# Where an interleaved weight decoder keeps its intermediate words, and in which slots it runs

## The chip, the core and the metric

The kernel runs on one core of a Trainium2 chip. The metric is the device time of one execution in microseconds (us); the median of the runs of the kernel before is 1018.41 us.

## What is computed

Attention over 4 batches, 8 heads, 576 rows of 64 feeds a rational feed-forward layer, and that feeds a layer of eight routed experts. The change sits between the first two. Cut to that:

```python
scores = scale * q @ k.T                       # 4 x 8 x 576 x 576
scores = where(scores >= max - tau, scores, -1e9)
x = softmax(scores) @ v                        # rows of 512: x is 2304 x 512
h = x @ w_in                                   # 2304 x 2048
g = (a0 + a1*h + a2*h^2 + a3*h^3) / (1 + |b0|*|h| + |b1|*h^2 + 1e-6)
y = g @ w_out                                  # 2304 x 512
# then: gate by argmax, one of 8 experts (512 -> 1024 -> 512) per row
```

`w_in` and `w_out` arrive as 64-bit floats. [...]

## The kernel before

**Tiling.** `x` stands transposed in SBUF as 18 tiles of 128 rows. The feed-forward layer works in 96 chunks: a chunk is one group of three row tiles (`SEGS`) with one of 16 pieces of 128 hidden columns. A chunk's first product is 12 matmuls (L945), its second is 9 (L1017), five slots later (`G_LAG`). Chunks go in pairs through the rational function: ACT lines L968 to L970, POOL L971, ACT L980 and L981, DVE L959 to L961, ACT L998, POOL L999, and DVE L973 and L974. The PSUM tile of a pair's first product comes back with L961 of that pair; there are two such tiles.

**Slots.** `moe1` is a generator that advances one slot at a time. Slots 0 to 51 stand beside the last 52 of the 144 attention steps (`PRE`), slots 52 to 56 beside attention's end, and chunk c has slot 53 + c. Slot 54 is cut in three (`HALVES`), so that hooks at 54.5 and 54.75 fall between pieces of attention's end. Slot 57 (`END`) opens the pools of `w_out`'s split pieces and the last two PSUM banks (`ps_b`); slot 52 opens `ps_h` (the first products) and `ps_a` (two banks for sums of second products).

**Decoding.** The weights come in 32 pieces of 128 x 512 values, in the order of `STREAM`: (0, n) is piece n of `w_in`, (1, n) of `w_out`. A piece is loaded by an SP DMA into `raw`, its exponent is scaled by ACT (L621), and `step` runs three DVE operations: the low word's last bits (L618), the merge (L624), the sign (L628, into a `mag` tile). `sign` also issues the next load. The first eight pieces do this in place, `raw` to `raw` to `mag`, all in SBUF; from the ninth on (`late`) the intermediate words stand in one PSUM bank (`aux`), and for `w_out` POOL takes the last bits (L616) three slots ahead. A decoded `w_in` piece is summed (L800), the sums of two pieces go through a matmul (L809) and a row of tiny DVE operations (L634 to L653) to a scale, POOL makes factors of it (L834 to L839), and the piece is split in two halves of a product (ACT L846 and L847, or L849 and POOL L850; then POOL L851). A `w_out` piece is split by ACT L856 and POOL L857.

**What sets the order.** Every engine runs its queue in the order in which the program was written out, and that is set by tables: `FIRST_AT` (slots in which the first eight pieces are done), `EARLY_STEPS` (the three DVE operations of the first two pieces apart), `FIRST_EXPONENTS`, `EARLY_SUM` (the scale of pieces 0 and 1), `DEC_AT` and `DEC_EVERY` (a later piece every 1.6 slots from slot 59). Hooks of one slot run in a fixed order behind that slot's chunk work.

Of the kernel before, what the change touches and what calls it, by code (L numbers as in the profile page):

```python
# [13 lines left out]
I32 = mybir.dt.int32  # L14
# [39 lines left out]
END = 57  # L54
# [3 lines left out]
IN_LOAD = (8, 12, 33, 37, 41, 52, 52)  # L58
COEFFICIENTS = 30
STREAM = ((0, 0), (0, 1), (0, 2), (0, 3), (1, 0), (1, 1), (1, 2), (1, 3), (0, 4), (0, 5), (0, 6), (0, 7), (1, 4), (1, 5), (1, 6), (1, 7), (0, 8), (0, 9), (0, 10), (0, 11), (1, 8), (1, 9), (0, 12), (0, 13), (1, 10), (1, 11), (0, 14), (0, 15), (1, 12), (1, 13), (1, 14), (1, 15))  # L60
EARLY_STEPS = ((19, 21, 25), (27, 31, 33))
EARLY_SUM = 35
FIRST_AT = (25, 33, 52, 53, 55, 57, 57, 58)
FIRST_EXPONENTS = (17, 25, 46, 48, 50, 56, 56, 57)
SHIFT_LEAD = 3
SECOND_SUM = 54
HALVES = (54,)
DEC_AT = 59
DEC_EVERY = 1.6


def decode_at():
# [11 lines left out]
OUT_LAG = 1  # L84
# [582 lines left out]
def moe1(nc, tc, xT, vs, w_in, w_out, a, bb, w_gate, w_ogate, gates, ident, yd, part, L, consts, keep, side, early_bank):  # L667
# [43 lines left out]
    def at(slot, f, *args):  # L711
        hooks.setdefault(max(slot, 0), []).append((f, args))
# [7 lines left out]
    def run(slot):  # L720
        order = (load_next, last_bits, exponent, sum_in, red_in, clamp_red, split_out, split_in, scale_in, factors_in)
        for f, args in sorted(hooks.pop(slot, ()), key=lambda x: order.index(x[0]) if x[0] in order else -1 - (x[0] in early)):
            f(*args)
# [17 lines left out]
    def late(key):  # L741
        return key not in STREAM[:len(FIRST_AT)]

# [11 lines left out]
    def aux():  # L755

        if not aux_b:
            aux_b.append(bank(3))
        return aux_b[0]
# [9 lines left out]
    def step_parts(key):  # L769
        now = {}  # L770

        def bits():
            raw, t = raws[key], mags.pop(key, None)
            low, high = raw[:, :, 0], raw[:, :, 1]
            out = mags[key] = mag_buf(key[0])
            if t is not None:
                high = t.bitcast(I32)
                t = high
            elif late(key):
                t = aux().bitcast(I32)  # L780
                dec.last_bits(raw, t)
                low = t
            else:
                t = out.bitcast(I32)
                dec.last_bits(raw, low)
            now.update(t=t, high=high, low=low, out=out)

        def merge():
            dec.merge(now["t"], now["high"], now["low"])

        def sign():
            dec.sign(now["out"].bitcast(I32), raws.pop(key)[:, :, 1], now["t"])
            if key not in STREAM[:2]:
                load_next()

        return bits, merge, sign
# [63 lines left out]
    end = decode_at()  # L860
# [11 lines left out]
    for m in GROUPS:  # L872
        if n < 2 * m:
            for i in range(n, n + m):
                at(end[0, i] + (i != 2), sum_in, i)
            t = SECOND_SUM if n else EARLY_SUM
            at(t + 0.5, red_in, n, m, True)
            at(t + 0.75, clamp_red, n, m)
            at(t + 0.75, scale_in, n, m)
            for i in range(m):  # L880
                at(t + (0.8, 1)[i] if n else t + 2 + 2 * i, split_in, n + i)
            at(t + 1, factors_in, n, m)
        else:
            for i in range(n, n + m):
                at(end[0, i] + 1, sum_in, i)
            t = max(end[0, i] for i in range(n, n + m)) + 1
            at(t + 1, red_in, n, m)
            at(t + SC_LAG, scale_in, n, m)
            at(t + SC_LAG, factors_in, n, m)
            for i in range(m):  # L890
                at(t + IN_LAG + i * SPLIT2, split_in, n + i)
        n += m
    for n in range(NFC):
        at(max(end[1, n] + OUT_LAG, END), split_out, n)
    queue = list(STREAM)
    for t in IN_LOAD:
        at(t, load_next)
# [105 lines left out]
    def bank(i):  # L1003
        return (ps_a if i < 2 else ps_b[0]).tile([P, DM], F32, tag=f"b{i}", name="acc")
# [168 lines left out]
    for t in range(PRE, START + len(chunks) + G_LAG):  # L1173
        if t == END:
            open_wo()
            open_wo()
            d2_p.append(pool("d2", 1))
            ps_b.append(pool("ps_b", 1, space=PSUM))
            nc.sync.dma_start(out=gates[:, :, 0:E], in_=w_gate.rearrange("(k p) e -> p k e", p=P))
            nc.sync.dma_start(out=gates[:, :, E:2 * E], in_=w_ogate.rearrange("(k p) e -> p k e", p=P))  # L1180
        c = t - START
        fill = chains(t) + side.fill(t)
        if 0 <= c < len(chunks) + 2:
            emit_in(c, fill)
        else:
            for f in fill:
                f()
        if G_LAG <= c < len(chunks) + G_LAG:
            emit_out(c - G_LAG)
        if len(chunks) <= c < len(chunks) + UN:  # L1190
            side.first_products(c - len(chunks), half_tile)
        if t in hooks:
            run(t)
        if t < END:
            yield
        for x in ((0.5,), (0.75, 0.8)) if t in HALVES else ():
            for y in x:
                run(t + y)
            yield
# [690 lines left out]
```

## Time and profile before

| | |
|---|---|
| runs (us) | 1018.41, 1018.55, 1016.29; median 1018.41 |
| the profiled execution's own time | 1022.82 us |
| its span, first to last instruction | 1020.8 us |
| busy in the span (us) | PE 938.0, DVE 797.8, ACT 680.4, POOL 542.8 |

| stretch (us) | what runs | PE busy | DVE | ACT | POOL | granted clock |
|---|---|---|---|---|---|---|
| 250 to 275 | attention, slots 24 to 36 | 21.89 | 22.59 | 20.42 | 20.27 | 0.99 |
| 325 to 350 | chunks 5 to 8 | 18.62 | 23.11 | 16.70 | 13.31 | 0.86 |
| 350 to 375 | chunks 9 to 14, decoding | 24.65 | 22.71 | 21.33 | 17.42 | 1.00 |
| 375 to 400 | chunks 15 to 19, decoding | 22.35 | 18.11 | 18.53 | 24.36 | 1.00 |
| 500 to 525 | chunks 42 to 46 | 21.00 | 14.37 | 14.09 | 15.15 | 0.86 |

Times in the trace are counted from the span's start. A row of the timeline has the start, the duration, the engine, the line of the program, the operation, its output and inputs, and in brackets the idle time of the engine just before it with what ended it. A clock of 1.00 is TensorE at full speed.

### The profile page before, as it was taken

What the parts mean: (1) busy time and instruction counts of PE and PEld (TensorE: products, weight loads), DVE (VectorE), ACT (ScalarE), POOL (GpSimd) and SP (SyncE); (2) the same over time, 40 slices, a digit from 0 to 9 for tenths busy, and PEclk for the clock granted to TensorE, in tenths of its full rate; (3) what the DMA queues carried; (4) which work ended last, traced back from release to release, by engine and by line L of the source; (5) the groups of instructions that cost most, each with busy time, mean ns of one, the idle gap of its engine ahead of it and who ended that gap; (6) DMA issues with size and microseconds to landing.
All of it is one profiled execution on the core that took longest, in us unless ns stands there. A gap on an engine that the chain in (4) does not pass through costs nothing.

```text
span 1020.8 us, 20731 instructions
## 1 busy us (share of the span) xinstructions
PE 938.0 (92%) x7899; PEld 687.2 (67%) x7899; DVE 797.8 (78%) x1337; ACT 680.4 (67%) x1006; POOL 542.8 (53%) x540
## 2 busy tenths in 40 slices
PE   8898899998887898999799999998788999999996
PEld 5565666665555565666466666665567899999995
DVE  5897899999997988888658878998983986555652
ACT  5888888887886687878666566656553555455552
POOL 2687688888794488697854344444341132111120
PEclk9999999999999899999899999999999999999998
DMA  9999999999996432322003212032123011111340
GB/s 211 179 211 197 199 185 186 184 187 207 178 179 168 134 114 94 114 83 74 0 1 93 73 53 63 32 93 74 42 52 135 22 63 42 42 42 42 119 130 24
DMA packets 234188, 110.26 MB, mean 108 GB/s; under 512 B 196832, under 2 KB 221408, under 8 KB 234080
## 3 DMA queue, kind: packets, MB, share of 16 engines
q1 hardware_dynamic: 230816, 98.89, 45.0%
q0 software_dynamic: 3120, 9.96, 3.0%
q8 instruction: 64, 1.05, 0.4%
q14 instruction: 44, 0.36, 0.1%
q10 hardware_dynamic: 144, 0.00, 0.0%
HBM read 82.61 MB, written 13.63 MB: 94 GB/s over the span
## 4 chain that ended last, share of the span: by engine, by line
PE 48%; DVE 20%; POOL 11%; issue 10%; ACT 8%; DMA 2%; SPq 0%; POOLq 0%; ACTq 0%; DVEq 0%
PE h L1690 10%; PE o L1707 9%; PE h L945 6%; PE acc L1017 6%; PE s L357 5%; PE tp L207 5%; PE xps L415 4%; POOL t L971 3%; DVE e L381 3%; POOL gl L999 2%; DVE t L959 2%; DVE h L960 2%; POOL raw L616 2%; POOL wol L857 1%; DMA pt<-php 1%
## 5 line engine op out<-in xcount | busy, mean ns | idle before, releaser
L387 POOL TENSOR_TENSOR php<-e,php 128x512 f16<-128x512 f32 x144 | 166.7, 1162 | 66.7 <-ACT php L385 65.0
L971 POOL TENSOR_TENSOR t<-t,ah 128x768 f32<-128x768 f32 x48 | 87.9, 1830 | 176.8 <-ACT t L970 169.9
L945 PE MATMUL h<-xT,wih 128*128 128x384 f16 x768 | 145.4, 334 | 30.2 <-DVE s L961 18.4
L945 PEld LDWEIGHTS <-wih 128*128 128x128 f16 x768 | 68.7, 99 | 94.8 <-DVE s L961 26.4
L1017 PE MATMUL acc<-woh,gh 128*128 128x512 f32 x288 | 126.9, 441 | 3.8 <-ACT woh L856 2.7
L369 ACT ACTIVATE e<-s,mn 128x576 f32<-128x576 f32 x144 | 106.8, 742 | 33.9 <-DVE mn L368 30.2
L357 PE MATMUL s<-kt,qT 64*128 64x256 f32 (+3 forms) x640 | 116.9, 457 | 5.8 <-DVE mn L374 5.0
L381 DVE SCALAR_TENSOR_TENSOR e<-s,mn,e 128x576 f32<-128x576 f32 x144 | 116.6, 810 | 6.1 <-ACT e L369 6.1
L1717 POOL DMA_INDIRECT out_dram<-os,sidx x19 | 24.6, 1293 | 181.4 <-ACT os L1716 151.0
L1017 PE MATMUL acc<-wol,gh 128*128 128x512 f32 x288 | 115.5, 401 | 3.1 <-POOL wol L857 3.1
L415 PEld LDWEIGHTS <-pt 128*128 128x128 f16 (+1 forms) x2240 | 79.1, 101 | 55.5 <-issue 52.3
L1017 PE MATMUL acc<-woh,gl 128*128 128x512 f32 x288 | 115.4, 401 | 0.7 <-POOL gl L999 0.5
L368 DVE TENSOR_REDUCE mn<-s 128x1 f32<-128x576 f32 x144 | 107.9, 750 | 6.8 <-PE s L357 6.5
L385 ACT ACTIVATE php<-e 128x576 f16<-128x576 f32 x144 | 98.5, 684 | 4.7 <-DMA pt<-php 4.7
L999 POOL TENSOR_TENSOR gl<-s,gh 128x768 fp32r<-128x768 f32 x48 | 91.0, 1895 | 7.7 <-issue 4.9
L415 PE MATMUL xps<-vs__112,pt 128*128 128x65 f16 (+1 forms) x2240 | 93.5, 196 | 0.0
L980 ACT ACTIVATE h<-t,co 128x768 f32<-128x768 f32 x48 | 43.5, 906 | 63.7 <-POOL t L971 26.0
L945 PE MATMUL h<-xT,wil 128*128 128x384 f16 x384 | 80.6, 334 | 1.8 <-POOL wil L851 1.8
L968 ACT ACTIVATE ah<-h,cvs 128x768 f32<-128x768 f32 x48 | 43.3, 902 | 52.9 <-PE h L945 48.6
L959 DVE SCALAR_TENSOR_TENSOR t<-t,co,h 128x768 f32<-128x768 f32 x48 | 48.5, 1010 | 29.5 <-POOL gl L999 16.6
L1017 PEld LDWEIGHTS acc<-woh,gh 128*128 128x128 f32 x288 | 55.4, 192 | 18.4 <-ACT woh L856 3.4
L1650 DVE TENSOR_TENSOR wol<-xT,woh 128x1024 fp32r<-128x1024 f32 x45 | 56.8, 1270 | 13.5 <-ACT woh L1649 13.0
(390 smaller groups left out, 2326.3 us busy)
## 6 DMA issues: line engine op xcount, KB each, us to landing
xT<-in_moe_w_dram SPq DMA_DIRECT2D x80, 512.0 KB
raw<-in_moe_w_in_dram SPq DMA_DIRECT2D x16, 512.0 KB
raw<-in_moe_w_out_dram SPq DMA_DIRECT2D x16, 512.0 KB
yd<-y SPq DMA_DIRECT2D x18, 256.0 KB
raw<-in_k_dram SPq DMA_DIRECT2D x16, 256.0 KB
raw<-in_q_dram SPq DMA_DIRECT2D x16, 256.0 KB
xT<-in_v_dram SPq DMA_DIRECT2D x8, 512.0 KB
part<-part SPq DMA_DIRECT2D x15, 256.0 KB
```

What stands on the lines that cost most here:

```text
L357: nc.tensor.matmul(ps[po:po + m, o:o + n], qT[r, g % 2, hh, t, po:po + m], KT[g][r, bb, c:c + n], start=True, stop=True)
L368: nc.vector.tensor_reduce(mn[:, n:n + 1], st[i], axis=AX.X, op=ALU.min)
L369: nc.scalar.activation(e[:, n], st[i], AF.Exp, bias=mn[:, n:n + 1], scale=-1.0)
L381: nc.vector.scalar_tensor_tensor(e[:, n], st.pop(i), mn[:, 2 + n:3 + n], e[:, n], op0=ALU.is_le, op1=ALU.mult)
L385: nc.scalar.activation(hi, e[:, n], AF.Copy)
L387: nc.gpsimd.tensor_tensor(lo[:, b:b + 512], e[:, n, a:a + 512], hi[:, a:a + 512], op=ALU.subtract)
L415: nc.tensor.matmul(x, pt[:, blk, po:po + m], vv[:, par, hh, j, :], start=False, stop=(i % 6 == 5 and n == 13))
L945: nc.tensor.matmul(hb[:, 0:n], w_cols(w, fc)[:, k], xT[:, k, t0:t0 + TR, lo, :], start=(i == 0), stop=(i == 11))
L971: nc.gpsimd.tensor_tensor(t1, t1, ah, op=ALU.mult)
L999: nc.gpsimd.tensor_tensor(gl, s, gh.bitcast(F32), op=ALU.subtract)
L1017: nc.tensor.matmul(acc[r, i], g[:, i * P:(i + 1) * P], w, start=first and m == 0, stop=last and m == 2)
L1690: self.nc.tensor.matmul(hp[:, a], w[:, k, a], x[:, k], start=(k == 0 and m == 0), stop=(k == K1 - 1 and m == 2))
```

## The change

Seven edits:

- Pieces 3 to 8 of the stream no longer decode in SBUF: their intermediate words go to a PSUM bank, one of the two of `ps_a` in slots 52 to 55 and `aux` from slot 57 on.
- The middle steps of the first two pieces move by a slot: L624 of the first from 21 to 22, and all three of the second from 27, 31, 33 to 28, 31, 34.
- The first piece's exponent moves from slot 17 to 14, the second's from 25 to 26.
- The scale of pieces 0 and 1 moves from slot 35 to 38, with its two splits (37 and 39 to 40 and 42).
- `w_in` piece 3 is split in the hook of slot 54 instead of slot 55.
- `w_out` piece 0 is split ahead of slot 57's chunk work instead of behind it.
- From slot 59 on a piece is decoded every 1.52 slots instead of 1.6: 59, 60, 62, 63, 65, 66, 68, 69 and so on to 93, where it was 59, 60, 62, 63, 65, 67, 68, 70 and so on to 95. The sums, scales, splits and loads hang on these slots and move with them.

```diff
-EARLY_STEPS = ((19, 21, 25), (27, 31, 33))
-EARLY_SUM = 35
-FIRST_AT = (25, 33, 52, 53, 55, 57, 57, 58)
-FIRST_EXPONENTS = (17, 25, 46, 48, 50, 56, 56, 57)
+EARLY_STEPS = ((19, 22, 25), (28, 31, 34))
+EARLY_SUM = 38
+FIRST_AT = (25, 34, 52, 53, 55, 57, 57, 58)
+FIRST_EXPONENTS = (14, 26, 46, 48, 50, 56, 56, 57)
...
-DEC_EVERY = 1.6
+DEC_EVERY = 1.52
...
-            elif late(key):
-                t = aux().bitcast(I32)
+            elif key not in STREAM[:2]:
+                t = (aux() if ps_b else bank(key[1] % 2)).bitcast(I32)
...
-                at(t + (0.8, 1)[i] if n else t + 2 + 2 * i, split_in, n + i)
+                at(t + 0.8 if n else t + 2 + 2 * i, split_in, n + i)
...
-        at(max(end[1, n] + OUT_LAG, END), split_out, n)
+        at(max(end[1, n] + OUT_LAG, END) - (n == 0) / 2, split_out, n)
...
             nc.sync.dma_start(out=gates[:, :, E:2 * E], in_=w_ogate.rearrange("(k p) e -> p k e", p=P))
+            run(t - 0.5)
```

On DVE, at the end of attention (slots 52 and 53), the rows before are these; `raw` and `mag` are in SBUF, `xps` is attention's output sum:

```order
L381 SCALAR_TENSOR_TENSOR e<-s,mn,e 128x576
L618 TENSOR_SCALAR raw<-raw 128x512
L624 SCALAR_TENSOR_TENSOR mag<-raw 128x512
L628 SCALAR_TENSOR_TENSOR mag<-raw,mag 128x512
L618 TENSOR_SCALAR raw<-raw 128x512
L624 SCALAR_TENSOR_TENSOR mag<-raw 128x512
L628 SCALAR_TENSOR_TENSOR mag<-raw,mag 128x512
L425 RECIPROCAL rinv<-xps 128x6
```

And now; `acc` is a PSUM bank:

```order
L381 SCALAR_TENSOR_TENSOR e<-s,mn,e 128x576
L618 TENSOR_SCALAR acc<-raw 128x512
L624 SCALAR_TENSOR_TENSOR acc<-raw,acc 128x512
L628 SCALAR_TENSOR_TENSOR mag<-raw,acc 128x512
L618 TENSOR_SCALAR acc<-raw 128x512
L624 SCALAR_TENSOR_TENSOR acc<-raw,acc 128x512
L628 SCALAR_TENSOR_TENSOR mag<-raw,acc 128x512
L425 RECIPROCAL rinv<-xps 128x6
```

The place is the same, the tiles are others: each operation has at most one operand left in SBUF beside its output.

On ACT, around slot 57, before (L856 is `w_out` piece 0):

```order
L621 ACTIVATE raw<-raw 128x512 x2
L446 ACTIVATE xT<-tp 128x3x128
L446 ACTIVATE xT<-xps 128x3x128
L980 ACTIVATE h<-t,co 128x2x384
L981 ACTIVATE h<-h 128x2x384
L621 ACTIVATE raw<-raw 128x512
L856 ACTIVATE woh<-mag 128x512
L968 ACTIVATE ah<-h,cvs 128x768
```

And now:

```order
L621 ACTIVATE raw<-raw 128x512 x2
L446 ACTIVATE xT<-tp 128x3x128
L446 ACTIVATE xT<-xps 128x3x128
L856 ACTIVATE woh<-mag 128x512
L980 ACTIVATE h<-t,co 128x2x384
L981 ACTIVATE h<-h 128x2x384
L621 ACTIVATE raw<-raw 128x512
L968 ACTIVATE ah<-h,cvs 128x768
```

L856 has moved ahead of three operations.

On POOL, slots 62 to 66, before: two pairs' work (L971, L999) with what is queued up to the next L971:

```order
L971 TENSOR_TENSOR t<-t,ah 128x768
L999 TENSOR_TENSOR gl<-s,gh 128x768
L616 TENSOR_SCALAR raw<-raw 128x512
L971 TENSOR_TENSOR t<-t,ah 128x768
L999 TENSOR_TENSOR gl<-s,gh 128x768
L616 TENSOR_SCALAR raw<-raw 128x512
L834 TENSOR_TENSOR cvs<-sc,vs 128x2x2
L837 TENSOR_TENSOR cvs<-cvs 128x2x2
L839 TENSOR_SCALAR cvs<-cvs,co 128x2x2 x2
L616 TENSOR_SCALAR raw<-raw 128x512
L850 TENSOR_SCALAR mag<-mag,sc 128x512
L851 TENSOR_TENSOR wil<-mag,wih 128x4x128
```

And now:

```order
L971 TENSOR_TENSOR t<-t,ah 128x768
L999 TENSOR_TENSOR gl<-s,gh 128x768
L616 TENSOR_SCALAR raw<-raw 128x512 x2
L971 TENSOR_TENSOR t<-t,ah 128x768
L999 TENSOR_TENSOR gl<-s,gh 128x768
L834 TENSOR_TENSOR cvs<-sc,vs 128x2x2
L837 TENSOR_TENSOR cvs<-cvs 128x2x2
L839 TENSOR_SCALAR cvs<-cvs,co 128x2x2 x2
L616 TENSOR_SCALAR raw<-raw 128x512
L850 TENSOR_SCALAR mag<-mag,sc 128x512
L851 TENSOR_TENSOR wil<-mag,wih 128x4x128
```

One L616 has gone a pair ahead.

## Rows read from the trace of the kernel before

**Rows 1.** Timeline of PE, starts of first products: start, duration, operation, [idle before].

```profile
348.70 1.47 PE L945 MATMUL h<-xT,wih 128*128 128x384 f16 x8
...
491.24 1.47 PE L945 MATMUL h<-xT,wih 128*128 128x384 f16 x8 [1.26 <-DVE s L961]
495.30 1.47 PE L945 MATMUL h<-xT,wih 128*128 128x384 f16 x8
502.25 2.08 PE L945 MATMUL h<-xT,wih 128*128 128x384 f16 x8 [2.74 <-ACT wih L849]
...
510.57 1.47 PE L945 MATMUL h<-xT,wih 128*128 128x384 f16 x8
```

**Rows 2.** Timeline of POOL, L971 of the pairs of slots 64, 66 and 70.

```profile
366.09 1.84 POOL L971 TENSOR_TENSOR t<-t,ah 128x768 f32<-128x768 f32 x1 [2.29 <-issue]
...
376.97 1.83 POOL L971 TENSOR_TENSOR t<-t,ah 128x768 f32<-128x768 f32 x1
...
396.81 1.84 POOL L971 TENSOR_TENSOR t<-t,ah 128x768 f32<-128x768 f32 x1
```

**Rows 3.** Groups by line, 343 to 512 us: busy us, mean ns of one, idle before.

```profile
L616 POOL TENSOR_SCALAR raw<-raw 128x512 uint32<-128x512 uint32 x12 | 24.1, 2010 | 1.1
...
L961 DVE SCALAR_TENSOR_TENSOR s<-s,co,h 128x768 f32<-128x768 f32 x19 | 19.3, 1015 | 0.7
...
L857 POOL TENSOR_TENSOR wol<-mag,woh 128x512 fp32r<-128x512 f32 x12 | 15.4, 1286 | 6.6 <-ACT woh L856 6.5
...
L851 POOL TENSOR_TENSOR wil<-mag,wih 128x512 f16<-128x512 f32 x12 | 14.0, 1168 | 1.0
```

**Rows 4.** One line's instructions (L618, L624): duration ns min/median/max, first and last start.

```profile
L618 DVE TENSOR_SCALAR acc<-raw x12: 684/689/691, 341.7 to 474.5; 128x512 int32<-128x512 int32 x12
L618 DVE TENSOR_SCALAR raw<-raw x8: 418/450/750, 239.0 to 336.4; 128x512 int32<-128x512 int32 x8
...
L624 DVE SCALAR_TENSOR_TENSOR acc<-raw,acc x12: 696/696/697, 342.5 to 475.3; 128x512 int32<-128x512 int32 x12
...
L624 DVE SCALAR_TENSOR_TENSOR mag<-raw x8: 683/694/1640, 242.4 to 336.9; 128x512 int32<-128x512 int32 x8
```

**Rows 5.** Timeline of DVE, long decoding operations of slots 52, 57 and 58.

```profile
304.72 1.53 DVE L624 SCALAR_TENSOR_TENSOR mag<-raw 128x512 int32<-128x512 int32 x1
...
331.11 1.64 DVE L624 SCALAR_TENSOR_TENSOR mag<-raw 128x512 int32<-128x512 int32 x1
...
337.62 2.23 DVE L628 SCALAR_TENSOR_TENSOR mag<-raw,mag 128x512 int32<-128x512 int32 x1
```

**Rows 6.** Timeline of POOL beside the last of these.

```profile
337.47 1.83 POOL L999 TENSOR_TENSOR gl<-s,gh 128x768 fp32r<-128x768 f32 x1 [2.28 <-ACT gh L998]
```

**Rows 7.** Timeline of PE, slots 54 to 59.

```profile
311.82 0.59 PE L809 MATMUL tp<-tot,co 128*128 128x2 f32 x2 [2.52 <-ACT wih L800]
...
320.40 1.47 PE L945 MATMUL h<-xT,wih 128*128 128x384 f16 x8 [0.58 <-ACT wih L847]
...
336.50 1.46 PE L945 MATMUL h<-xT,wih 128*128 128x384 f16 x8 [0.56 <-DVE s L961]
...
341.03 0.50 PE L1017 MATMUL acc<-wol,gh 128*128 128x512 f32 x1 [2.06 <-POOL wol L857]
```

**Rows 8.** Timeline of DVE, slot 35, first operation behind the sum's matmul.

```profile
273.73 0.16 DVE L634 TENSOR_SCALAR t<-tp 128x2 f32<-128x2 f32 x1 [1.84 <-PE tp L809]
```

**Rows 9.** Timeline of ACT, attention at slots 14 and 17.

```profile
228.81 0.75 ACT L369 ACTIVATE e<-s,mn 128x576 f32<-128x576 f32 x1
...
235.03 0.68 ACT L385 ACTIVATE php<-e 128x576 f16<-128x576 f32 x1 [1.34 <-DMA pt<-php]
```

**Rows 10.** Timeline of SP's queue: the first piece's load.

```profile
226.73 0.58 SPq L609 DMA_DIRECT2D raw<-in_moe_w_in_dram  x1
```

**Rows 11.** Chain that ended last, 205 to 300 us: the transfer issued behind that load.

```profile
227.46 7.48 DMA pt<-php
```

## The prediction

> **What bounds the kernel now.** I read the table of stretches first, then the timelines of PE, POOL and DVE where PE is under 24 us in 25, and the chain of waits to see which idle time is on the path.
>
> From chunk 8 on PE sets the pace where nothing is late: chunk 40 starts at 491.24 and chunk 41 at 495.30, so a slot costs 4.06 us and a pair of slots 8.12 [rows 1]. From chunk 8 (348.70) to chunk 43 (510.57) are 35 slots; they take 161.87 us and would take 142.1, so 19.8 us are lost there. Of these 7.2 lie between chunk 41 and chunk 43 (15.27 us for two slots worth 8.12): chunk 42 is the first to use `w_in` piece 14, and waits 2.74 us for that piece's split (L849), then for the lower half behind it. The other 12.6 us I lay on POOL. From L971 of slot 64's pair to that of slot 66's are 10.88 us, and 19.84 for the next two pairs [rows 2], where PE would need 8.12 each. POOL has work queued ahead of each L971, and a late L971 means a late L961, a late PSUM tile and an idle PE (the 1.26 us ahead of chunk 40 is one such). Before chunk 8, at attention's end, PE, ACT and DVE wait for one another in turn. In attention's last third DVE is nearly always busy, so what it idles or works there counts.
>
> **The change, part by part.** *PSUM for pieces 3 to 8.* With PSUM words all L618 take 684 to 691 ns and all L624 696 to 697. In SBUF the medians are 450 and 694, but single ones reach 750 and 1640 [rows 4]. The long ones [rows 5] stand beside POOL work: L628 at 337.62 runs to 339.85, 0.55 us past the end of POOL's L999, which began just before it [rows 6]. So the shift gets 0.24 us dearer in every decode, and the merge and the sign fall from up to 2.23 to 0.70.
>
> [...]
>
> The way through attention's end: slot 52's decode is on the path. Its merge takes 1.53, its sign as long; both fall to 0.70, less 0.35 for the shift and its gap: 1.3 us. ACT's sum waits for it, and the matmul that waits 2.52 us for that sum comes 1.3 earlier (311.82 in [rows 7]). Chunk 3 waits 0.58 for `w_in` piece 3's split (320.40 in [rows 7]); split in the hook before, while ACT waits for PE anyway, that goes: 1.9 so far. In slot 57 the merge of 1.64 falls to 0.70, less 0.35: 2.5 at L961, and so at chunk 6, which waits for it (336.50 in [rows 7]). [...] So chunk 8 comes 3.0 us earlier. The early copy of `w_out` piece 0 I cost at nothing: PE gets to its second product sooner, but chunk 6 still needs L961, and what hides the copy is DVE's two decodes of slot 57; without them it could bring up to the 0.6 that the copy takes on ACT. Bounds of this part: 0.9 if only piece 3's split and a quarter of the first decode count, 4.5 if PE no longer falls to its lower clock there (0.86 in the table's stretch).
>
> *The scale at slot 38.* DVE stands 1.84 us at slot 35, since the matmul waits for a PSUM tile that ACT is still copying out [rows 8]. At slot 38 that tile has been free for a step; the matmul then needs only the two attention products ahead of it on PE, which run while DVE does its three operations of the step. I leave 0.2. Gain 1.6, bounds 0 and 1.84.
>
> *The exponent at slot 14.* ACT reaches it where L369 now starts, at 228.81 [rows 9], but its load is issued only at 226.73, SP's queue being in order and behind [rows 10]. The transfer issued after the load lands at 227.46 + 7.48 = 234.94 [rows 11]; the load lands between 227.3 and that. Halfway, at 231.1, ACT stands 2.3 us, and behind it wait DVE's L381, POOL's L387 and the transposes that SP issues from them. But ACT now stands 1.34 us for that later transfer at 235.03 [rows 9], and 0.6 of exponent leaves slot 17, on the chain there. Net 0.4 lost; bounds 0.6 gained and 4.5 lost. The one-slot moves of the first two pieces keep DVE's work and pass no other queue: 0, within 0.5 either way.
>
> *Every 1.52 slots.* This frees piece 14: its partner's decode goes from slot 89 to 87 and its split from slot 94 to 92, so 8.1 us sooner, more than the 7.2 lost there. All 7.2 go if POOL keeps up. POOL's price from its queue: L971 and L999 3.7 a pair, an L616 2.01, an L857 1.29 [rows 3]. With what was queued in slots 64 to 69, rows 2 give 1.7 for an L851 with its scaling and 1.5 for the factors with their gaps. Over 8.12 us the pairs of slots 64, 66, 68 had 6.4 together; those of 78, 80, 88, 92, 94 had 0.3, 2.0, 3.0, 1.6, 0.3: 13.6 in all, the last 1.9 under the wait for piece 14. The rest, 11.7, against 12.6 lost: overruns do turn into idle PE, with 0.9 from elsewhere. Now the pairs of 64, 66, 68 have 0.8, 3.3, 0.3 and those of 78, 80, 86, 90, 92 have 1.3, 3.0, 3.0, 1.6, 0.3: again 13.6. With the 0.9 the loss is 14.5. DVE gets two `w_in` pieces in one pair four times instead of once: five operations of 1.0 [rows 3] and two decodes of 2.1 [rows 4] make 9.3, over by 1.2. Two of the three new ones fall where POOL is over anyway; for that of slot 74 I take 0.6. So 19.8 becomes 15.1: gain 4.7, bounds 7.2 and a loss of 2. The loads behind each sign come at most two slots sooner, on an SP queue with nothing else in these slots.
>
> Sum: 3.0 + 1.6 - 0.4 + 4.7 = 8.9 us off the profiled span of 1020.8 (its execution took 1022.82, 4.4 above the median). From the median of 1018.4: 1009.5.
>
> **Rivals.** *Dense decoding gives much of it back.* DVE's overruns add to POOL's instead of lying under them, 3 x 1.2 less 0.6, and the double L616 of slot 74 delays the next L971 by its own 2.0: 5.0 together, 1014.5. For it: DVE works 22.7 us of 25 in 350 to 375 already. Against it: before L971 of slot 64 POOL idles 2.29 [rows 2], room for one more L616.
>
> *ACT waits for the load.* If the load lands with the transfer behind it, 4.5 is lost instead of 0.4: 1013.6. For it: SP's lag. Against it: the load is ahead in the queue.
>
> *Slower: POOL never catches up.* Between 366 and 397 its pairs took 10.2 us. If all fifteen from slot 64 to 93 took that, 15 x 2.1 = 31.5 would be lost instead of 19.8; with the other gains of 4.2 that is 7.5 slower, 1025.9. It decides once the loss passes 24. Against it: pairs with one L857 or nothing (slots 70, 72, 82) stand between.
>
> *Piece 14 stays late*, its split still stuck behind ACT's or POOL's queue: 4.7 turns to -0.6, 1014.8.
>
> *More than forecast*: PE keeps its full clock through attention's end (1.5), the load has landed (1.0), DVE's overrun is absorbed (0.6): 1006.4.
>
> **How the numbers follow.** 1009.5 is forecast with 0.58 (1007 to 1012.5); dense decoding has 0.10, ACT's wait 0.09, piece 14 still late 0.05, slower 0.07, more than forecast 0.11. About 0.3% (3.1 us) is what a measurement here can tell from no change. Below 1015.3 lie the forecast, the larger gain, and most of the other three faster ones: 0.82. Within 0.3%: 0.11. Slower: 0.07. The range runs from 1004 to 1016: it takes in the cheaper rivals and leaves out the slower one and the tails.
>
> **What would show it.** L624 and L628 of pieces 3 to 8 at 0.70, none above 0.8, confirm the first term, with chunk 8 some 4 us earlier (1.2 of that from attention). L634 with under 0.5 us idle ahead of it confirms the second. Chunk 42 without a wait for L849 confirms the last; intervals of 11 to 12 us between L971 at slots 66, 80 and 86 price it. An L621 on ACT near 229 with several us idle ahead of it, ended by a DMA, would show the second rival; idle PE well above 15 us between chunks 8 and 43 the first or the third. The forecast is wrong if that loss grows by more than chunk 42's wait.

## The result and the profile after

The changed kernel's runs took 1013.9, 1007.58, 1009.8, 1004.17 and 1008.82 us: median 1008.82, beside 1016.44 for five of the kernel before. The ratio is 0.9915, 95% interval 0.9887 to 0.9943, so 7.6 us faster. 1009.5 was forecast, 8.9 off the 1018.41 of the first three runs of the kernel before; all five of them have the median 1016.44. The traced execution is the longest of the five (1013.9, span 1011.9). Line numbers are those of the kernel before up to L1181, and one higher behind it.

TensorE's timeline of the changed kernel, with the starts of chunks 0, 2, 3, 6, 8, 41, 42 and 43 and the column sum of attention's end; answers to [rows 1] and [rows 7]:

```profile
302.49 1.46 PE L945 MATMUL h<-xT,wih 128*128 128x384 f16 x8 [0.24 <-DVE mn L374]
...
310.53 0.38 PE L809 MATMUL tp<-tot,co 128*128 128x2 f32 x2 [1.23 <-ACT wih L800]
...
314.15 1.47 PE L945 MATMUL h<-xT,wih 128*128 128x384 f16 x8
316.98 1.46 PE L945 MATMUL h<-xT,wih 128*128 128x384 f16 x8
...
332.57 1.76 PE L945 MATMUL h<-xT,wih 128*128 128x384 f16 x8 [3.60 <-DVE s L961]
...
344.39 1.47 PE L945 MATMUL h<-xT,wih 128*128 128x384 f16 x8
...
493.20 1.47 PE L945 MATMUL h<-xT,wih 128*128 128x384 f16 x8
497.53 1.46 PE L945 MATMUL h<-xT,wih 128*128 128x384 f16 x8
501.57 1.47 PE L945 MATMUL h<-xT,wih 128*128 128x384 f16 x8
```

Chunk 0 starts where it did before (302.50). Chunk 8 comes 4.3 us sooner, chunk 43 another 4.7: chunk 8 to chunk 43 takes 157.18 us where it took 161.87. From there to the end both kernels take the same within 0.2. Chunk 42 waits for no split, and chunk 41 to chunk 43 takes 8.37 instead of 15.27.

DVE's decoding operations by line in the changed kernel (duration in ns, least, median, greatest); answers to [rows 4]:

```profile
L618 DVE TENSOR_SCALAR acc<-raw x18: 683/687/698, 304.4 to 464.6; 128x512 int32<-128x512 int32 x18
L624 DVE SCALAR_TENSOR_TENSOR acc<-raw,acc x18: 695/696/706, 305.1 to 465.3; 128x512 int32<-128x512 int32 x18
L628 DVE SCALAR_TENSOR_TENSOR mag<-raw,acc x30: 686/686/703, 305.8 to 493.0; 128x512 int32<-128x512 int32 x30
```

None of those with words in PSUM is longer than 0.706 us; the 1.53, 1.64 and 2.23 of [rows 5] are gone. In attention L634 has no wait left, and ACT stands 0.29 us for the first load (timelines of DVE and of ACT; [rows 8], [rows 9]):

```profile
276.72 0.15 DVE L634 TENSOR_SCALAR t<-tp 128x2 f32<-128x2 f32 x1
```

```profile
230.09 0.68 ACT L621 ACTIVATE raw<-raw 128x512 f32<-128x512 f32 x1 [0.29 <-DMA raw<-in_moe_w_in_dram]
```

POOL's timeline, L971 of the pairs of slots 66 and 68, 80 and 82, 86 and 88 ([rows 2] have it of before):

```profile
370.48 1.84 POOL L971 TENSOR_TENSOR t<-t,ah 128x768 f32<-128x768 f32 x1
381.63 1.83 POOL L971 TENSOR_TENSOR t<-t,ah 128x768 f32<-128x768 f32 x1
...
433.54 1.86 POOL L971 TENSOR_TENSOR t<-t,ah 128x768 f32<-128x768 f32 x1
445.43 1.81 POOL L971 TENSOR_TENSOR t<-t,ah 128x768 f32<-128x768 f32 x1
...
462.11 1.85 POOL L971 TENSOR_TENSOR t<-t,ah 128x768 f32<-128x768 f32 x1 [0.38 <-ACT t L970]
473.99 1.81 POOL L971 TENSOR_TENSOR t<-t,ah 128x768 f32<-128x768 f32 x1
```

The intervals are 11.15, 11.89 and 11.88, where the account of POOL's queue had 11.4, 11.1 and 11.1. POOL itself idles only 0.3 to 0.5 us in each.

### The profile page after: what moved, and what is told of

It reads as the page before. It is cut to its first block, busy times and chain, and to the rows that moved or that the text cites. A ratio compares the mean times of both kernels' runs of the same rounds, so it can differ in the third digit from the quotient of the medians.

```text
span 1011.9 us, 20733 instructions
## 1 busy us (share of the span) xinstructions
PE 935.0 (92%) x7899; PEld 685.9 (68%) x7899; DVE 795.1 (79%) x1337; ACT 679.8 (67%) x1006; POOL 540.8 (53%) x540
## 5 line engine op out<-in xcount | busy, mean ns | idle before, releaser
L971 POOL TENSOR_TENSOR t<-t,ah 128x768 f32<-128x768 f32 x48 | 87.9, 1830 | 177.5 <-ACT t L970 174.6
L1017 PE MATMUL acc<-woh,gh 128*128 128x512 f32 x288 | 126.8, 440 | 1.8 <-ACT part L1034 1.7
L369 ACT ACTIVATE e<-s,mn 128x576 f32<-128x576 f32 x144 | 107.1, 744 | 31.4 <-DVE mn L368 27.9
L381 DVE SCALAR_TENSOR_TENSOR e<-s,mn,e 128x576 f32<-128x576 f32 x144 | 116.2, 807 | 5.3 <-ACT e L369 5.2
L1718 POOL DMA_INDIRECT out_dram<-os,sidx x19 | 24.1, 1268 | 179.8 <-ACT os L1717 150.1
L1017 PE MATMUL acc<-wol,gh 128*128 128x512 f32 x288 | 115.1, 400 | 1.9 <-POOL wol L857 1.9
L1017 PE MATMUL acc<-woh,gl 128*128 128x512 f32 x288 | 114.6, 398 | 1.9 <-POOL gl L999 1.9
L415 PEld LDWEIGHTS <-pt 128*128 128x128 f16 (+1 forms) x2240 | 78.5, 101 | 53.5 <-issue 50.2
L385 ACT ACTIVATE php<-e 128x576 f16<-128x576 f32 x144 | 98.6, 685 | 4.8 <-DMA pt<-php 2.8
L999 POOL TENSOR_TENSOR gl<-s,gh 128x768 fp32r<-128x768 f32 x48 | 91.0, 1897 | 7.0 <-issue 4.6
L415 PE MATMUL xps<-vs__112,pt 128*128 128x65 f16 (+1 forms) x2240 | 92.9, 196 | 0.0
L1017 PEld LDWEIGHTS acc<-woh,gh 128*128 128x128 f32 x288 | 55.2, 192 | 16.2 <-ACT part L1034 2.1
```

What stands on the lines that cost most here:

```text
L369: nc.scalar.activation(e[:, n], st[i], AF.Exp, bias=mn[:, n:n + 1], scale=-1.0)
L381: nc.vector.scalar_tensor_tensor(e[:, n], st.pop(i), mn[:, 2 + n:3 + n], e[:, n], op0=ALU.is_le, op1=ALU.mult)
L385: nc.scalar.activation(hi, e[:, n], AF.Copy)
L415: nc.tensor.matmul(x, pt[:, blk, po:po + m], vv[:, par, hh, j, :], start=False, stop=(i % 6 == 5 and n == 13))
L971: nc.gpsimd.tensor_tensor(t1, t1, ah, op=ALU.mult)
L999: nc.gpsimd.tensor_tensor(gl, s, gh.bitcast(F32), op=ALU.subtract)
```

## Why two traces can't be subtracted whole

Attention looks as if it had gained nothing. Step by step (starts of DVE's L381, the steps numbered like the slots beside them) the changed kernel is 2.9 us ahead at step 40 and level at step 43. Stretches of its trace: length, then busy us of PE, its weight loads, DVE, ACT and POOL with the number of instructions in brackets, then the granted clock, DMA share and GB/s:

```profile
278.00:280.00 2.00, 0.93 (x7) 0.53 (x4) 1.97 (x6) 1.35 (x2) 1.79 (x4) 0.74 1.08 202
280.00:282.00 2.00, 2.00 (x20) 1.22 (x19) 2.00 (x5) 1.40 (x3) 1.92 (x3) 0.50 0.84 236
282.00:284.00 2.00, 2.00 (x24) 1.14 (x25) 1.63 (x4) 1.97 (x4) 1.92 (x6) 0.50 1.29 153
```

TensorE's granted clock was 0.50 there, and four score matmuls took 1.44 us where they take 0.81 at 1.00. The same kernel traced once more (after_again) has, over the same steps:

```profile
274.00:276.00 2.00, 0.97 (x18) 0.48 (x14) 2.00 (x11) 1.02 (x3) 2.00 (x2) 1.00 1.15 215
276.00:278.00 2.00, 1.52 (x19) 0.92 (x19) 1.97 (x5) 1.13 (x3) 1.79 (x4) 1.00 0.85 147
278.00:280.00 2.00, 1.75 (x34) 1.30 (x34) 2.00 (x6) 1.97 (x4) 1.84 (x7) 1.00 1.99 255
```

So the traces are compared stretch by stretch, and over several kernels that share the stretch.

## The experiments

**One part alone, and the changed kernel again.** The three parts are edits of the kernel before; psum_part has the edits at attention's end:

```diff
-            elif late(key):
-                t = aux().bitcast(I32)
+            elif key not in STREAM[:2]:
+                t = (aux() if ps_b else bank(key[1] % 2)).bitcast(I32)
...
-                at(t + (0.8, 1)[i] if n else t + 2 + 2 * i, split_in, n + i)
+                at(t + 0.8 if n else t + 2 + 2 * i, split_in, n + i)
...
-        at(max(end[1, n] + OUT_LAG, END), split_out, n)
+        at(max(end[1, n] + OUT_LAG, END) - (n == 0) / 2, split_out, n)
...
+            run(t - 0.5)
```

> The kernel before with the PSUM edit, piece 3's split a quarter of a slot sooner and the early copy of w_out piece 0 alone. Theory 1 (the term of the prediction, as the two traces put it): chunk 8 comes about 4.3 us sooner than in the kernel before relative to chunk 0, chunk 0 is where it was, everything behind chunk 8 keeps its intervals, so chunk 43 and the end are 3 to 4.3 us earlier: near 1012.7. Rival A (the stretch after it takes it up: the stages behind are bound by DVE and POOL, not by when they begin): chunk 8 is 4 us sooner, but chunk 43 less than 1 us: within 1 us of before. Rival B (the shorter intervals between chunks 0 and 8 come from the earlier decoding every 1.52 slots, not from PSUM): chunk 0 to chunk 8 as before, 46.2 us.

Measured: 1014.72 (ratio 0.9979, 0.9960 to 0.9998). Chunk 0 to chunk 8 takes 42.89, 3.3 less than in the trace of before, and chunk 8 to chunk 41 as there (146.65 and 146.60), so both rivals are out. The median is 3.0 under that of the kernel before run beside it, 2.1 by the ratio, where 3 to 4.3 was expected. In this trace L415 stood 0.84 us for a late transfer ahead of chunk 2, which no other has.

```diff
-EARLY_STEPS = ((19, 21, 25), (27, 31, 33))
-EARLY_SUM = 35
-FIRST_AT = (25, 33, 52, 53, 55, 57, 57, 58)
-FIRST_EXPONENTS = (17, 25, 46, 48, 50, 56, 56, 57)
+EARLY_STEPS = ((19, 22, 25), (28, 31, 34))
+EARLY_SUM = 38
+FIRST_AT = (25, 34, 52, 53, 55, 57, 57, 58)
+FIRST_EXPONENTS = (14, 26, 46, 48, 50, 56, 56, 57)
```

> The kernel before with the moved steps, the sum's row at slot 38 and the exponents at slots 14 and 26 alone. Theory 1 (clock): the moves bring 2 to 3 us by 280 us, and the changed kernel's trace lost them between 279 and 286 because TensorE's granted clock fell to half there (L357 took up to 0.90 us instead of 0.43); that fall depends on where PE stood idle just before and need not come in every execution: chunk 0 between 299.5 and 302.5, the median 1 to 3 us under before's. Rival A (fixed schedule): the gain is always given back before chunk 0, since in attention's last steps something else (DVE's queue, or ACT's splits of slots 40 and 42) sets the time: chunk 0 at 302.5 within 0.3, median within 1 us of before. Rival B (loss): ACT's earlier exponent and the fuller last steps cost something: chunk 0 later than 303, the median over before's.

Measured: 1018.06 (1.0014, 0.9992 to 1.0037). The median fits rival A, no gain. In the trace chunk 0 starts at 299.06, and TensorE's clock fell only once in attention, at 115 us (the step from 114.0 takes 5.08 us), as theory 1 has it; its median, 1 to 3 us under, did not come. The table below takes this up.

```diff
-DEC_EVERY = 1.6
+DEC_EVERY = 1.52
```

> The kernel before with decoding every 1.52 slots alone. Theory 1 (the prediction's term): chunk 42 no longer waits for L849, chunk 8 to chunk 43 takes 157.2 us instead of 161.9, 4.7 us less as in the changed kernel: near 1012. Rival A (it needs the PSUM edit): with chunk 8 some 4 us later and w_in's words in SBUF, dense decoding overruns POOL and DVE more: chunk 8 to chunk 43 takes 160 or more, gain under 2 us. Rival B (piece 14's wait was all that could be won): 7.2 us off, 154.7.

Measured: 1012.96 (0.9948, 0.9924 to 0.9971). Chunk 42 waits for nothing; chunk 8 to chunk 43 takes 158.45, 3.4 less than in the trace of before. It doesn't need the PSUM edit, so rival A is out, and rival B's 154.7 too.

> The changed kernel once more, to see what differs between two of its executions. Theory 1 (clock): its executions spread by several us because the stretches in which TensorE runs at half its clock come at other places or are fewer; an execution with a mean granted clock of 0.985 is 4 to 6 us shorter than the one of 0.979 traced before (1011.9 of span), and if this trace has no such stretch between 279 and 286 us, chunk 0 comes at about 299.5 instead of 302.5. Rival (another cause, such as DMA queues): chunk 0 and the intervals differ by several us between the two traces where the granted clock is the same.

Measured: 1008.92 (0.9924, 0.9897 to 0.9951). Clock 0.985, chunk 0 at 297.50; chunk 1 to 2, chunk 5 to 6 and chunk 41 to 43 within 0.01 us of the first trace. Of the 5.0 us at chunk 0, 2.5 are there by step 13 and 1.9 come between steps 34 and 43. The clock fell at 26 and 118 us in the first trace (granted 0.55 to 0.60 and 0.51 to 0.64 over 4 us), at 94 in this one (two steps behind it take 5.82 us, 4.35 in the first trace): step by step these falls make 1.1 of the 2.5. Theory 1 holds for the 1.1 and the 1.9, and for 1.7 more between chunks 0 and 8, where the first trace has twice as long a stretch at half the clock (0.50 from 334 to 340 us). The other 2.0 come without any fall, as the rival has it: 0.6 before the first L381, 0.7 near 80 us, 0.6 between steps 18 and 34. What makes them is open.

**Without the moves in attention; the sum alone back.** psum_pace is the changed kernel with the diff of attention_part undone, sum_back is

```diff
-EARLY_SUM = 38
+EARLY_SUM = 35
```

> The changed kernel without its moves in attention (the steps of the first two pieces, the sum's row and the exponents stand as in the kernel before). Theory 1 (attention's moves bring at most 0.6 us where TensorE's clock does not fall, as the four traces so far put it step by step): median within 2 us of the changed kernel's 1008.9, and the steps from 201 us to chunk 0 take the same as in the kernel before run with the PSUM edit alone, within 0.3. Rival (they were worth the 1.2 us of the prediction or more, and the run of them alone lost it by chance): 1010 to 1013.

> The changed kernel with the sum's row back at slot 35. Theory 1: from attention's step 34 to step 35 it takes 2.8 us more than in the changed kernel (4.27 against 1.51), since L634 waits for the matmul again, and of these 2.8 the steps 36 to 43 give back 1.5 to 2.2, because what stood at slot 38 (scale, factors, two splits) no longer stands there; by chunk 0 the difference is 0.6 to 1.3 us. Rival A (the prediction's term): 1.6 us and more are left at chunk 0. Rival B: nothing or less than nothing is left, since the later splits of pieces 0 and 1 hold up attention's last steps.

Measured: 1011.23 (0.9940, 0.9919 to 0.9960) and 1009.46 (0.9940, 0.9916 to 0.9963). The medians don't settle what the moves are worth: 2.3 and 0.5 over after_again, inside the intervals. Theory 1 of psum_pace missed: its median lies in the rival's range, and from its step 0 to chunk 0 it takes 3.0 us more than psum_part with the same program there (101.6 and 98.6; 2.0 of it at step 17, 0.9 between steps 34 and 43). So one trace doesn't settle it either; several, step by step, show more. This table has the time between starts of L381, for thirteen traces of which all share the last column:

| trace | exponent at | sum at | steps 13 to 17 | 17 to 18 | 18 to 34 | 34 to 43 | 43 to 51 |
|---|---|---|---|---|---|---|---|
| before | 17 | 35 | 7.66 | 3.09 | 33.52 | 18.85 | 13.74 |
| psum_part | 17 | 35 | 7.66 | 1.73 | 33.52 | 18.19 | 13.73 |
| pace_part | 17 | 35 | 7.66 | 1.73 | 33.50 | 18.25 | 13.73 |
| psum_pace | 17 | 35 | 7.66 | 3.73 | 33.57 | 19.13 | 13.74 |
| fill_wait | 17 | 35 | 7.66 | 3.20 | 33.51 | 19.14 | 13.73 |
| piece_14 | 17 | 35 | 7.65 | 1.73 | 33.51 | 18.40 | 13.73 |
| sum_back | 14 | 35 | 7.66 | 1.50 | 33.00 | 20.03 | 13.74 |
| after | 14 | 38 | 7.66 | 1.51 | 33.64 | 19.44 | 13.75 |
| after_again | 14 | 38 | 7.66 | 1.51 | 33.00 | 17.57 | 13.74 |
| attention_part | 14 | 38 | 8.36 | 1.51 | 33.78 | 17.58 | 13.74 |
| copy_back | 14 | 38 | 8.09 | 1.51 | 33.31 | 18.77 | 13.75 |
| spread | 14 | 38 | 7.66 | 1.50 | 33.20 | 17.57 | 13.75 |
| lumped | 14 | 38 | 7.66 | 1.50 | 33.05 | 17.58 | 13.75 |

With the sum at slot 35, steps 34 to 43 take 18.19 where the clock stays up (psum_part) and up to 20.03 where it falls (sum_back); at slot 38, 17.57 where it stays up, 18.77 and 19.44 where it falls. So the move brings 0.6 with the clock up (a single trace on the one side) and 0.8 on average (18.86 and 18.09): it fell there in two of six traces with the sum at 38, in six of seven with it at 35. sum_back's step 34 to 35 takes 3.1 us more than after_again's (2.8 was expected), and by chunk 0 it is 2.6 behind. That is rival A's number, but 1.84 of it is what its steps 34 to 43 take more than psum_part's, which has the sum in the same place and no fall; the rest is theory 1's.

**Matmuls in the wait.** In the kernel before, ahead of the sum in `sum_rows`:

```diff
+        if key == 2:
+            for _ in range(40):
+                nc.tensor.matmul(ps, ident.bitcast(F16)[:, 0:P], ident.bitcast(F16)[:, 0:P], start=True, stop=True)
```

> The kernel before, with 40 matmuls of 128 columns put on TensorE ahead of the column sum L809 of attention's end, into the PSUM tile that this sum then overwrites: they run while TensorE would stand 2.5 us for ACT's L800, and change no result. Theory 1 (the fall of TensorE's clock near 310 us follows that wait, and is a part of what the wait costs): there is no stretch at half the clock between chunks 1 and 2, L415 and L207 behind L809 take what they take in the changed kernel, and chunk 1 to chunk 2 takes 10.9 to 11.2 us instead of 12.40 to 12.55, though the wait itself is still there. Rival A (the PSUM edit kept the clock up in another way, or chance did): the fall comes as before, 12.4 to 12.6. Rival B: the matmuls hold up L809 by as much as they save.

TensorE's timeline of fill_wait (its lines are 3 higher from the sum on), up to the start of chunk 2:

```profile
308.33 2.39 PE L810 MATMUL tp<-ident 128*128 128x128 f16 x40
311.13 0.38 PE L812 MATMUL tp<-tot,co 128*128 128x2 f32 x2 [0.41 <-ACT wih L800]
...
311.54 2.47 PE L415 MATMUL xps<-vs__112,pt 128*128 128x65 f16 x70
313.94 0.88 PE L207 MATMUL tp<-ident,xf 128*64 128x128 f32 x12
314.75 1.48 PE L948 MATMUL h<-xT,wih 128*128 128x384 f16 x8
```

and of pace_part, where the wait stands as in the kernel before:

```profile
309.96 0.38 PE L809 MATMUL tp<-tot,co 128*128 128x2 f32 x2 [2.53 <-ACT wih L800]
...
310.37 3.32 PE L415 MATMUL xps<-vs__112,pt 128*128 128x65 f16 x70
313.62 1.50 PE L207 MATMUL tp<-ident,xf 128*64 128x128 f32 x12
315.05 1.47 PE L945 MATMUL h<-xT,wih 128*128 128x384 f16 x8
```

The sum waits for ACT as long as ever, yet L415 takes 2.47 instead of 3.32 and L207 0.88 instead of 1.50: chunk 1 to chunk 2 takes 11.12 us, against 12.40 to 12.55 in the four traces with that wait unfilled. In all four the granted clock fell to half behind it (0.50 from 312 to 314 us in the trace of before, from 310 to 312 in piece_14; L415 takes 3.32 to 3.54 in the four), in none of the eight with the PSUM edit, where the wait is 1.23 or 1.24 (in the changed kernel's trace it is 1.00 from 310 to 316 and L415 takes 2.47), nor in fill_wait (1.00 from 308 to 318). Theory 1 holds for this place, in the one trace taken. The whole execution shows no gain from 1.3 us in one place: 1017.84 (1.0005, 0.9979 to 1.0031).

**The early copy undone.** The changed kernel with

```diff
-        at(max(end[1, n] + OUT_LAG, END) - (n == 0) / 2, split_out, n)
+        at(max(end[1, n] + OUT_LAG, END), split_out, n)
```

> The changed kernel without the early copy of w_out piece 0 to ACT (it stands in slot 57 as before). Theory 1 (the prediction's: worth nothing): the first matmul of the second product waits some 2.7 us for L856 instead of 1.3 us for L857 behind it, but chunk 6 waits for DVE's L961 either way, so chunk 5 to chunk 6 takes 9.64 us within 0.1, and chunk 8 comes as in the changed kernel. Rival: L961's chain is reached through ACT's queue (L968 to L970 stand behind the copy), and chunk 5 to chunk 6 takes 10.1 to 10.3, the 0.6 of the copy more.

TensorE's timeline of copy_back, the second product of chunk 0 and the start of chunk 6:

```profile
325.52 0.49 PE L1017 MATMUL acc<-woh,gh 128*128 128x512 f32 x1 [2.22 <-ACT woh L856]
326.87 0.50 PE L1017 MATMUL acc<-wol,gh 128*128 128x512 f32 x1 [0.85 <-POOL wol L857]
...
330.82 2.72 PE L945 MATMUL h<-xT,wih 128*128 128x384 f16 x8 [1.19 <-DVE s L961]
```

The wait for L856 is 2.22 where some 2.7 was expected. What PE waits ahead of the second product it doesn't wait ahead of chunk 6: chunk 5 to chunk 6 takes 9.63 as with the copy, chunk 0 to chunk 8 40.19 as in after_again (40.18). In this place the copy is worth nothing. Median 1009.56.

**Three pieces sooner.** The kernel before, with

```diff
-    return dict(zip(STREAM, FIRST_AT)) | {key: DEC_AT + int(DEC_EVERY * i) for i, key in enumerate(STREAM[n:])}
+    return dict(zip(STREAM, FIRST_AT)) | {key: DEC_AT + int(DEC_EVERY * i) for i, key in enumerate(STREAM[n:])} | {(1, 11): 85, (0, 14): 86, (0, 15): 87}
```

> The kernel before with three pieces decoded one or two slots sooner and nothing else: w_in 14 in slot 86 instead of 87, 15 in 87 instead of 89, w_out 11 in 85 instead of 86; all others every 1.6 slots as before. Theory 1 (of the edit to 1.52 all that helps is that piece 14 comes in time; the rest of the denser decoding only moves POOL's overruns): chunk 42 waits for no split, chunk 41 to 43 takes 8.1 to 8.6 us instead of 13.5 to 15.3, POOL's overrun grows by 1.7 us before it, and chunk 8 to chunk 43 takes 157 to 158.5, as with 1.52. Rival A (the denser decoding costs on its way): 155 to 156. Rival B (the denser decoding helps on its way): 160 or more.

Measured: 1011.88 (0.9950, 0.9917 to 0.9983), as the edit to 1.52 alone. TensorE's timeline, chunks 41 to 44:

```profile
490.86 1.47 PE L945 MATMUL h<-xT,wih 128*128 128x384 f16 x8
495.18 1.46 PE L945 MATMUL h<-xT,wih 128*128 128x384 f16 x8
499.24 1.47 PE L945 MATMUL h<-xT,wih 128*128 128x384 f16 x8
...
505.77 1.48 PE L945 MATMUL h<-xT,wih 128*128 128x384 f16 x8 [1.26 <-DVE s L961]
```

Chunk 8 to chunk 43 takes 156.06: by the stretch that had been put down, that is rival A's number. But an overrun comes right behind it: chunk 43 to chunk 44 takes 6.53 instead of 4.06. From chunk 8 to chunk 45 it is 166.66, pace_part's 166.57, and up to chunk 95, the last, 402.2 in both. So theory 1 holds when counted further, an end that was chosen after the trace had been seen: the rest of the denser decoding neither helps nor harms, in one trace each.

**POOL's work spread, and in lumps.** If POOL's overruns are the loss, they should follow a table. In the changed kernel's place, a table of slots for the 24 pieces behind the eighth, chosen so that no pair of slots goes far over (lumped: the same with other numbers, so that pairs do):

```diff
-DEC_EVERY = 1.52
+LATE_AT = (59, 60, 62, 63, 65, 66, 68, 70, 71, 73, 74, 76, 77, 79, 80, 82, 83, 85, 86, 89, 91, 92, 97, 98)
...
-    return dict(zip(STREAM, FIRST_AT)) | {key: DEC_AT + int(DEC_EVERY * i) for i, key in enumerate(STREAM[n:])}
+    return dict(zip(STREAM, FIRST_AT)) | dict(zip(STREAM[n:], LATE_AT))
```

`STREAM`'s order behind the eighth piece goes with it.

> The changed kernel with other slots and another order for the 24 pieces behind the eighth, by a table: w_in 4 to 15 in slots 59, 60, 62, 63, 68, 70, 74, 77, 79, 80, 85, 86, w_out 4 to 15 in slots 65, 66, 71, 73, 76, 82, 83, 89, 91, 92, 97, 98. Nothing is decoded more seldom in all, w_in's piece 15 comes a slot sooner than in the changed kernel. Theory 1 (POOL's queue sets the loss between chunks 8 and 41: per pair of slots what it has to do over 8.12 us is idle PE): with L971 and L999 at 3.7 a pair, an L616 2.0, an L857 1.3, an L850 with L851 1.8 and the factors 1.4, the pairs of slots 62 to 96 go over by 14.7 us in the changed kernel and by 3.4 here. So chunk 8 to chunk 41 takes 137 to 139 us instead of 148.8 to 149.2, with POOL's interval between two L971 never over 10, and the median is 9 to 11 under the changed kernel's: near 999. Rival A (DVE's or ACT's queue sets it, the number of decodes being the same): chunk 8 to chunk 41 stays at 147 or more, median at 1008. Rival B (the earlier and later decodes wait for buffers or loads, so the table is not what happens): some decodes come late, chunk 42 or a second product waits; 143 to 147.

> As the table that spreads POOL's work, with the same first and last slots, but put so that POOL's work lies in lumps: w_in 4 to 15 in slots 59, 60, 62, 63, 66, 68, 74, 77, 79, 81, 83, 86, w_out 4 to 15 in slots 65, 69, 71, 72, 75, 85, 89, 90, 93, 94, 97, 98. By the same account the pairs of slots 66, 68, 72, 82, 86, 90 and 94 go over 8.12 us, by 22 us together, of which 20 before chunk 41 or 42. Theory 1 (POOL's queue): chunk 8 to chunk 43 takes 162 to 167 us (157.2 in the changed kernel, 142.1 with PE never idle), so the median is 5 to 9 over the changed kernel's, 1014 to 1018. Rival A (the number of decodes decides, not where they stand): as the spread table and the changed kernel, 157 within 2.

Measured: spread 998.87 (0.9831, 0.9812 to 0.9850), lumped 1018.65 (1.0020, 1.0000 to 1.0040). TensorE's timeline of spread, chunks 8, 41 and 43:

```profile
338.52 1.47 PE L945 MATMUL h<-xT,wih 128*128 128x384 f16 x8
...
479.16 1.47 PE L945 MATMUL h<-xT,wih 128*128 128x384 f16 x8
...
487.27 1.47 PE L945 MATMUL h<-xT,wih 128*128 128x384 f16 x8
```

and of lumped, chunks 8 and 43:

```profile
339.59 1.47 PE L945 MATMUL h<-xT,wih 128*128 128x384 f16 x8
...
504.03 1.47 PE L945 MATMUL h<-xT,wih 128*128 128x384 f16 x8
```

With the same 24 decodes, chunk 8 to chunk 43 takes 148.75 in spread, 157.18 to 157.59 in the changed kernel, 164.44 in lumped. POOL's timeline of spread, the longest interval between two L971 (9.74, slots 68 to 70):

```profile
374.04 1.84 POOL L971 TENSOR_TENSOR t<-t,ah 128x768 f32<-128x768 f32 x1
383.78 1.86 POOL L971 TENSOR_TENSOR t<-t,ah 128x768 f32<-128x768 f32 x1
```

and of lumped, slots 68 and 70, 72 and 74 (11.88 and 11.16; the account's prices give 11.3 and 11.5; from slots 86 and 90 it is 13.10 and 13.31):

```profile
375.55 1.85 POOL L971 TENSOR_TENSOR t<-t,ah 128x768 f32<-128x768 f32 x1
387.43 1.81 POOL L971 TENSOR_TENSOR t<-t,ah 128x768 f32<-128x768 f32 x1
394.23 1.82 POOL L971 TENSOR_TENSOR t<-t,ah 128x768 f32<-128x768 f32 x1 [1.96 <-ACT t L970]
405.39 1.84 POOL L971 TENSOR_TENSOR t<-t,ah 128x768 f32<-128x768 f32 x1
```

In each of these POOL idles 0.3 to 0.5 us. Theory 1 holds in both directions, with two reservations. Spread's chunk 8 to chunk 41 took 140.6, not 137 to 139, so that its median met the forecast 999 is in part luck: the account gives 3.4 us of overrun, and 6.6 are lost up to chunk 43. The intervals from slots 64, 72, 78 and 88 are 0.7 to 1.3 over 8.12, and POOL idles 1.5 to 3.8 in each, so something else holds them, which was not followed up. And lumped's total is not POOL's alone: its clock fell in that stretch (near 452 us four L1017 in a row take 0.63 to 0.88, where those of the next chunks take 0.39 to 0.53), and one interval (12.49 from slot 84, where the account has 5.1) comes from a full buffer, on DVE's timeline:

```profile
445.62 0.69 DVE L628 SCALAR_TENSOR_TENSOR mag<-raw,acc 128x512 int32<-128x512 int32 x1 [5.29 <-POOL wil L851]
```

The sign of a fifth `w_in` piece waits there until POOL's L851 frees one of four `mag` tiles. Spread beats both kernels: 10.0 us under the changed kernel's 1008.9, or 9.5 by the ratios, as the two were run apart.

## Why the prediction was right, and which of its steps were not

**The time came out, and all four terms were off, in size or sign; that the errors cancelled is luck.** Taken over all traces the four come to 4.1, 0.8, 0.9 and 3.2, with 0.2 for the one-slot moves: 9.2 where 8.9 was forecast, and 7.6 and 8.8 are the differences of the medians. The 9.2 is no sharper than a microsecond or two: by their medians the three parts alone bring 3.0, -0.4 and 4.7, and of attention's 1.9 the run of those moves alone shows nothing (1.0014, 0.9992 to 1.0037).

*PSUM at attention's end: 3.0 forecast, 4.1 measured.* Chunk 0 to chunk 8 takes 44.6 to 46.2 us in the four traces with the words in SBUF and the wait unfilled (mean 45.0), 40.2 to 42.9 in the eight with the words in PSUM (mean 40.9). Slot 52 gave what was said: the sum's wait fell from 2.52 to 1.23. But with it went the fall of the clock behind it, another 1.3 to 1.4 us, which the prediction had left to its rival of a larger gain; fill_wait shows that this is where it belongs. Piece 3's split gave 0.73 (chunk 2 to 3 takes 2.83 instead of 3.56), and 0.48 of it went again at chunk 4, which now waits 0.43 for L961; that new wait was not foreseen. Chunk 6 gained 1.0 where 0.6 was put down, slot 58 some 0.45 where 0.5 was (chunk 6 to chunk 8 takes 10.10 instead of 10.53 to 10.57 where the clock costs nothing, and the wait for L857 is gone), and the copy nothing, as put down. The last 0.5 of the 3.0, for slot 58, was the author's estimate, which no run shows as put down; in its place the traces have that 0.45, and POOL's two L857 there at 2.97 us before, with the sign at 2.23, and at 2.52 in the changed kernel, with it at 0.69. attention_part, which keeps these words in SBUF, has decodes of 1.64 and 2.23 us beside POOL's L857 and L999, as the trace of before has [rows 5, rows 6], while no kernel with the PSUM edit has one above 0.71 with its words there.

*The sum at slot 38: 1.6 forecast, 0.6 measured with the clock up, 0.8 on average.* The wait of 1.84 went as said. What the step left out is what moves with the sum: the splits of pieces 0 and 1 now stand in slots 40 and 42 on ACT, ahead of L369, on which DVE waits. ACT's timeline of after_again:

```profile
278.73 0.71 ACT L846 ACTIVATE mag<-mag,sc 128x512 f32<-128x512 f32 x1
279.47 0.63 ACT L847 ACTIVATE wih<-mag 128x512 f16<-128x512 f32 x1
280.00 0.72 ACT L369 ACTIVATE e<-s,mn 128x576 f32<-128x576 f32 x1
```

and DVE's, its only waits over 0.2 us between 268 and 287:

```profile
280.76 0.82 DVE L381 SCALAR_TENSOR_TENSOR e<-s,mn,e 128x576 f32<-128x576 f32 x1 [0.36 <-ACT e L369]
...
284.81 0.82 DVE L381 SCALAR_TENSOR_TENSOR e<-s,mn,e 128x576 f32<-128x576 f32 x1 [0.48 <-ACT e L369]
```

These and two of 0.18 and 0.17 are 1.19 of idle time where psum_part has the one of 1.84: 0.65 less, and 0.6 was gained. With the sum at slot 35 the same two splits cost DVE no such wait (psum_part).

*The exponent at slot 14: 0.4 lost forecast, 0.9 gained on average (steps 13 to 18 take 9.4 to 11.4 with it at 17, 9.2 to 9.9 at 14).* The step that failed is the wait for the load, put halfway between its bounds at 2.3 us. In the seven traces with the exponent at slot 14 ACT stands 0 to 0.35 us for it in five, 0.90 in copy_back and 1.16 in attention_part; ACT's timeline of the last:

```profile
228.56 0.67 ACT L621 ACTIVATE raw<-raw 128x512 f32<-128x512 f32 x1 [1.16 <-DMA raw<-in_moe_w_in_dram]
```

Only these two reach DVE (steps 13 to 17 take 8.09 and 8.36 instead of 7.66): 0.16 lost on average. The two terms against it were nearer, and both too large. The 1.34 us for a later transfer [rows 9] was taken as a fixed cover; ACT stands at that place in three of the six traces with the exponent at 17, for 1.34 to 2.00 us (in fill_wait the profile puts it down to DVE's L381), and over all six it is 0.81. The 0.6 of exponent that leaves slot 17 is worth 0.22 (that step takes 1.73 with no late transfer, 1.51 without the exponent). No trace with the exponent at 14 has that wait; whether the move keeps it away or chance does, these runs don't show.

*Every 1.52 slots: 4.7 forecast, 4.7 between the two traces, 3.2 over all.* Here the number was in part right for a wrong reason. Of the 7.2 lost around chunk 42, 1.7 was the clock of the one execution traced, 0.50 to 0.74 from 502 to 510 us; the other three traces with that wait take 13.52 to 13.56 from chunk 41 to 43, not 15.27, so 5.2 was to be had. The loss ahead of chunk 41 grew by 2.1 on average, near the forecast of 2.5 (chunk 8 to chunk 41 takes 146.6 to 147.6 at 1.6, 148.7 to 150.1 at 1.52). Counted to chunk 45, those three take 168.9 on average, the six at 1.52 take 165.7. POOL's intervals, which carried the step, came as worked out, and the two tables show that this account can be turned around and used. What it left out, 1.0 to 1.8 us in each of the intervals from slots 72, 76 and 84, where POOL itself stands idle 2.7 to 5.8, was not followed up.

*Of the rivals,* denser decoding took 2.1 us, where the forecast had allowed it 2.5. POOL never saturated, no split came late, and ACT's wait for the load stayed under 1.2. Of the larger gain's three parts two came: the clock (1.3 to 1.4), and the load, which had landed or nearly so in five of seven traces.

## To carry to other kernels

When an off-path engine's queue overruns its period now and then, write down per period what it has queued and move work between periods: the same 24 decodes in other slots were worth 9 to 10 us, more than the seven edits. A removed wait on TensorE was worth more than its length where the clock fell behind it (1.29 us of wait at attention's end, and another 1.3 to 1.4 us), so look at the granted clock right behind each wait before pricing it. And move a step only with all that hangs on it: the sum's row was free to move, its splits were not.

## What had not been expected of the hardware

Two executions of one program agree to some 0.02 us over long stretches (steps 43 to 51 take 13.73 to 13.75 in thirteen traces) and differ by up to 13 in all (the 25 runs of the kernel before beside fill_wait lie between 1010.17 and 1023.62). Part of that is where TensorE's granted clock falls to half (0.50 from 280 to 284 us in the first trace of the changed kernel, 1.00 over the same steps in the second): 3.0 of the 5.0 us between the two at chunk 0. A fall cost up to 1.7 us where TensorE sets the pace and nothing where it waits: chunk 41 to chunk 43 takes 13.54 and 13.56 with a fall in psum_part (0.64 and 0.51 from 496 to 500 us) and attention_part, 13.52 without in fill_wait (1.00). Behind an idle time of 2.50 to 2.60 us ahead of L809 it came in four of four traces, behind 1.23 or 1.24 in none of eight; at the 2.72 to 2.75 ahead of chunk 42 in three of four. What decides it where it doesn't always come, these runs don't show.
